# Sketched attention and a gated convolution on one core: loads in a set order, a new computing order, and no filler matmuls in TensorE's gaps

## The chip, the cores and the metric

The kernel runs on one core of one Trainium2 chip. The metric is the device time of one execution in microseconds. The kernel before takes 61.66 us in the median of three runs (61.4 to 61.86). The profile is one more execution of the same program; its span, from the first to the last instruction, is 60.0 us.

The core has five engines that run side by side, each in its own strict order: TensorE (PE, matmuls; PEld is its loading of weights), VectorE (DVE), ScalarE (ACT), GpSimd (POOL) and SyncE (SP, which here only issues transfers). ACT issues some transfers too.

## The reference

There are 4 batches, 4 heads, 1088 positions and 32 numbers a head. Keys and queries are taken to 64 features, the outer product of two projections to 8 numbers. Attention is linear: `kv` sums over all positions of a batch, so no query of a batch can be finished before all its keys and values are in. Batches don't depend on each other.

```python
def phi(x):                                     # (b, h, s, 32) -> (b, h, s, 64)
    a = einsum('rd,bhsd->bhsr', S1, x)
    b = einsum('rd,bhsd->bhsr', S2, x)
    return einsum('bhsi,bhsj->bhsij', a, b).reshape(*x.shape[:-1], 64)
q_p, k_p = phi(q), phi(k)
kv  = einsum('bhsf,bhsd->bhfd', k_p, v)         # sum over all positions
z   = sum(k_p, axis=2)
x   = einsum('bhsf,bhfd->bhsd', q_p, kv) / (einsum('bhsf,bhf->bhs', q_p, z) + 1e-6)
# x as (batch, 1088, 128): a causal convolution of 5 taps gives the gate
gate = sigmoid(sum(conv_w[t] * x[s - 4 + t] for t in range(5)))
out  = ((x @ w_val) * gate) @ w_out
```

## The kernel before

The program is a list of steps. Every step is a function of a kind, a batch and an index, and the list `ORDER` is the order in which they are emitted; each engine runs its own steps in that order. Digits after a colon choose among seven PSUM banks. The kinds are:

- `lk`, `lq`, `lv`, `lo`, `ls`, `lw`: loads of k, q, v, the last 64 positions of v of each batch (`v_lo`), S1 and S2, the weights. `cn`: constants.
- keys: `kt` (DVE transposes k), `kp` (PE projects it by S), `ke` (ACT copies the projection to SBUF), `kd` and `ko` (the outer product, on DVE and on POOL), `kv` (PE sums over the positions), `pz`, `pv`, `pm`, `pe` (kv and z made into weights for the queries).
- queries: `qt` (DVE transposes q), `qp` (PE projects), `qc` (ACT copies), `qm`, `qr`, `qi`, `qn` (the denominator and its division), `qo` (outer product, on DVE or POOL), `qx` (PE transposes phi), `qe` (copy to SBUF), `nm` (PE: times kv), `xe` (copy).
- gated part: `hl` (halo for the convolution), `gt` (PE: convolution by diagonal matrices), `sg` (ACT: sigmoid), `vl` (PE: times w_val), `gv` (DVE: gate times value), `om` (PE: times w_out), `oe` (copy), `so` (store).
- `cn06` and `zz`: matmuls of zeros by zeros, whose results nobody reads; `zz07:2` is seven of them.

```python
ORDER = """
cn08 lk01 cn00 ls00 cn06:01 lk00 lo00 ls01 lk10 cn05 cn07 lw00
cn09 lk20 kt01 lv12 lv01 zz07:2 lv02 cn01 lv00 cn02 lv03 kt00
cn013 cn011 cn010 kp00:2 kt10 lq01 lo01 kp01:3 ke00 cn03:4 zz05:0 ke01
ko00 cn04 lk30 kd01 kp10:5 lv13 kp11:6 lv10 ko01 ke10 kd00 kt20
... # cut
"""
...
elif i == 6:                                    # cn06
    for t in range(9):
        mm(bank("cn", b, i, t % 2), zero[:, 0:P], zero)

def s_zz(b, i):
    for t in range(i):
        mm(bank("zz", b, i), zero[:, 0:P], zero)

def queue(kind, b, i):                          # which engine issues a transfer
    return nc.scalar if (kind, b, i) in ON_ACT else nc.sync

def load(kind, b, i, x, y, t0, n):
    queue(kind, b, i).dma_start(
        out=y[b][:, t0 * D : (t0 + n) * D],
        in_=x[b].rearrange("h (m t) d -> (h m) (t d)", m=M)[:, t0 * D : (t0 + n) * D],
    )
# k and q of batch 0 come in two transfers (256 and 288 KB), of the others in one (544 KB);
# v in four of 128 KB a batch.

def s_kt(b, u):                                 # batch 0 in two halves, the others at once
    ...
    nc.vector.transpose(o, i_)

def s_kp(b, u):                                 # PE: wq[0] holds S1 and S2, spread over the heads
    ... mm(o[64 * z : 64 * z + 64, :, c, :], lt, wq[0][:, 0:64])

def s_kd(b, u):                                 # DVE does the first KD[b][u] of 4 + u chunks
    if KD[b][u]:
        outer(nc.vector, b, u, 0, KD[b][u], kab_view(b, u))

def s_ko(b, u):                                 # POOL does the others
    if KD[b][u] < 4 + u:
        outer(nc.gpsimd, b, u, KD[b][u], 4 + u, kab[(2 * b + u) % 4])

def copy(kind, b, i, out, in_):                 # qe, xe and oe
    if (kind, b, i) in ON_DVE:
        nc.vector.tensor_copy(out=out, in_=in_)
    else:
        nc.scalar.copy(out=out, in_=in_)
...                                             # cut: QM_POOL, QN_POOL, QO_POOL choose POOL or DVE likewise
for item in ORDER:
    what, _, banks = item.partition(":")
    kind, b, i = what[:2], int(what[2]), int(what[3:])
    slot[kind, b, i] = [int(x) for x in banks]
    steps["const" if kind == "cn" else kind](b, i)
```

Transfers share eight completion semaphores, dealt out in the order of the list. A transfer is issued only when the one eight places before it has landed, and while it waits, the issuing engine's later instructions wait with it.

Of the kernel before, what the change touches and what calls it, by code (L numbers as in the profile page):

```python
# [24 lines left out]


ORDER = """
cn08 lk01 cn00 ls00 cn06:01 lk00 lo00 ls01 lk10 cn05 cn07 lw00
cn09 lk20 kt01 lv12 lv01 zz07:2 lv02 cn01 lv00 cn02 lv03 kt00
cn013 cn011 cn010 kp00:2 kt10 lq01 lo01 kp01:3 ke00 cn03:4 zz05:0 ke01  # L30
ko00 cn04 lk30 kd01 kp10:5 lv13 kp11:6 lv10 ko01 ke10 kd00 kt20
lv11 lq00 kv00 ko10 ke11 lq10 zz01:0 lw02 kv01 lw01 kd10 kd11
kp20:0 ko11 pv00 kp21:1 pz00 kt30 lq20 ke20 zz02:2 ko20 lv20 kv10
lv22 ke21 lv21 kv11 qt00 lv23 ko21 pm00:2 kd20 kd21 qt01 pv10
kp30:4 pz10 pe00 qt10 lv33 pm10:3 ke30 qp01:5 lv31 pe10 lq30 kd30
cn012 kp31:6 qc01 qp11:0 lv32 qm01 ke31 qt20 ko30 lv30 qp00:1 qc11
ko31 qr01 kv20 qc00 kd31 kv21 qi01 qm00 qm11 qn01 qr00 qp10:2
qo03 pz20 pv20 qi00 qt30 pm20:3 qn00 qc10 qx03:4 kv30 qo01 pe20
qe03 qm10 kv31 qr10 qi10 qp20:6 qo02 pz30 pv30 qn11 qo00 qx01:5
qn10 qo13 qx02:3 qc20 pm30:2 qo11 qe01 qp21:4 qm20 qe02 pe30 qx00:1  # L40
qo12 nm03:6 qc21 qx13:5 qe00 nm02:3 qo10 qm21 qp30:2 xe02 qr20 qe13
nm00:0 qi20 qp31:1 qc30 xe00 qn20 xe03 qx10:3 qm30 nm01:5 qc31 qx12:0
qe10 qo20 nm13:6 xe01 qx11:2 qm31 xe13 nm10:3 gt00:51 qr30 qe12 hl00
qn21 xe10 qe11 qo21 gt01:60 sg00 qi30 sg01 vl02:3 qo23 vl00:2 sg03
nm12:5 qx20:1 sg02 gv00 nm11:0 qn31 xe12 qx23:4 gv02 qx21:6 xe11 qo22
qe23 vl03:2 vl01:5 qe21 gt10:30 gv01 hl10 gv03 nm23:4 qn30 sg11 om00:65
qe20 qx22:2 qo33 sg10 xe23 vl11:0 oe02 nm20:1 vl10:3 oe00 qe22 om01:5
so04 nm21:4 gv10 xe20 nm22:2 qo31 qx33:6 oe01 so00 xe21 gt11:31 so01
gv11 so02 gt20:45 sg12 xe22 qo30 sg13 so03 qe33 vl13:0 vl12:3 sg20
om10:21 gv13 sg21 qx31:6 gv12 qo32 oe12 qx30:4 oe10 qe31 nm33:0 so14  # L50
vl20:5 vl21:1 xe33 om11:3 gv20 nm31:2 so11 qe30 hl20 qx32:6 oe11 gt21:05
xe31 so10 qe32 gv21 hl30 nm30:4 so12 sg23 vl23:2 om20:36 xe30 sg22
nm32:1 so13 vl22:5 oe22 oe20 gt30:04 gv22 so24 gv23 so20 vl30:6 xe32
vl31:3 sg30 om21:5 so21 sg31 gt31:21 gv30 oe21 gv31 vl33:0 vl32:4 sg33
so22 om30:65 sg32 gv33 so23 oe30 gv32 oe32 om31:31 so30 so31 oe31
oe33 so34 so32 so33
""".split()


# [1 line left out]
def kernel(  # L61
# [25 lines left out]
    def st(name, shape, dt=F32):  # L87
        return sb.tile(shape, dt, tag=name, name=name)
# [23 lines left out]
    xe = [st(f"xe{i}", [P, 4 + NT, M], BF16) for i in range(3)]  # L112
# [163 lines left out]
    def kab_view(b, u):  # L276
        return bank("kp", b, u)[:, 0 : 2 * (4 + u) * 32].rearrange("p (k c x) -> p k c x", k=2, c=4 + u)
# [125 lines left out]
    def s_qn(b, U):  # L403
        pool = (b, U) in QN_POOL
        n = 4 * (5 - U)
        (nc.gpsimd if pool else nc.vector).tensor_mul(
            an[b % 2][:, rows(U), :], qa(b, U, 0, pool), bc(den[b % 2][:, rows(U)], 2, [P, n, 8])
        )

    def s_qo(b, g):  # L410
        U = g // 2
        lo = 8 * (g % 2)
        n = 12 if g == 1 else 8
        pool = (b, g) in QO_POOL
        a_ = an[b % 2][:, 20 * U + lo : 20 * U + lo + n, :]
# [95 lines left out]
    def s_so(b, g):  # L511
# [11 lines left out]

    KD = [[0, 4], [0, 3], [0, 0], [3, 2]]
    QM_POOL = {(0, 1), (1, 1)}
    QN_POOL = {(0, 0), (1, 0), (2, 0), (3, 0), (3, 1)}
    QO_POOL = {
        (0, 1), (0, 2), (0, 3), (1, 0), (1, 1), (2, 0), (2, 1), (2, 2), (3, 0), (3, 1), (3, 2), (3, 3),  # L530
    }
    ON_DVE = {
# [3 lines left out]
    }  # L536
    ON_ACT = {
        ('lk', 0, 0), ('lk', 0, 1), ('lk', 1, 0), ('lq', 0, 1), ('lv', 0, 2), ('lv', 0, 3),
        ('lv', 1, 1), ('lv', 1, 2), ('lw', 0, 2), ('so', 0, 1), ('so', 2, 4), ('so', 3, 0),
        ('so', 3, 2),  # L540
    }
    steps = {n[2:]: f for n, f in locals().items() if n.startswith("s_")}
# [35 lines left out]
```

## Time and profile before

| | before |
|---|---|
| time, median of 3 runs | 61.66 us |
| span of the profile | 60.0 us |
| PE busy | 47.5 us, 79% |
| weight loads (PEld) | 36.6 us, 61% |
| DVE busy | 39.5 us, 66% |
| ACT busy | 28.8 us, 48% |
| POOL busy | 35.4 us, 59% |
| read from HBM | 6.85 MB |
| written to HBM | 2.23 MB |
| zero matmuls on PE | 24, 8.3 us busy, 493 ns each |

The page gives busy time by engine, then cuts the span into 40 slices of 1.5 us and gives for each engine the share that it was busy, in tenths; PEclk is the clock granted to TensorE. The chain of waits follows the work that ended last back to what released it. The windows give busy time by engine for stretches that one chooses. Matmul records overlap one another, so their starts are a better measure than their lengths. A matmul of f32 leaves two records.

### The profile page before, as it was taken

The numbers are of one execution on the slowest core, as the hardware profiler recorded it, in microseconds if no ns is written. First come the engines' busy times: TensorE is split into PE (matmuls) and PEld (weight loads), VectorE is DVE, ScalarE is ACT, GpSimd is POOL, SyncE is SP. The second block draws the span as 40 slices with busy tenths as digits, with TensorE's granted clock in tenths as the row PEclk, the third lists the DMA queues.
The fourth block names the chain that finished last, engine by engine and source line by source line (L and its number), as shares of the span: only waits on it lengthen the run. The fifth ranks groups of instructions, "written<-read, shape, count | busy, mean of one in ns | idle before, by whom it ended". The sixth has DMA issues, their size and how long they took to land.

```text
span 60.0 us, 2668 instructions
## 1 busy us (share of the span) xinstructions
PE 47.5 (79%) x1129; PEld 36.6 (61%) x1129; DVE 39.5 (66%) x88; ACT 28.8 (48%) x83; POOL 35.4 (59%) x62
## 2 busy tenths in 40 slices
PE   1999709999704699999999999999999999962000
PEld 0333108587501687899888889988699797731000
DVE  1053089995399406696698796898799899964000
ACT  0540004940530005536356298999686999792000
POOL 4980052998399980008999988499999921000000
PEclk9999999999999555579999999999999999999955
DMA  0798999989999759300000000000000843897960
GB/s 0 195 285 277 352 340 262 256 282 358 404 378 340 225 146 376 126 0 0 11 0 0 11 0 5 11 5 0 16 0 22 262 116 82 193 238 164 242 186 3
DMA packets 6998, 9.25 MB, mean 154 GB/s; under 512 B 2117, under 2 KB 4682, under 8 KB 6986
## 3 DMA queue, kind: packets, MB, share of 16 engines
q1 hardware_dynamic: 5370, 6.69, 36.9%
q10 hardware_dynamic: 1616, 2.39, 13.0%
q8 instruction: 9, 0.15, 0.9%
q14 instruction: 3, 0.02, 0.1%
HBM read 6.85 MB, written 2.23 MB: 151 GB/s over the span
## 4 chain that ended last, share of the span: by engine, by line
PE 56%; DMA 29%; SPq 2%; ACTq 2%; ACT 2%; issue 1%
PE ring L140 36%; DMA q_in<-in_q_dram 11%; PE kv L140 9%; DMA s2raw<-in_S_dram 9%; DMA v_in<-in_v_dram 9%; PE ring L431 8%; PE ring L343 2%; ACT osb L231 2%; SPq L238 1%; ACTq L257 1%; SPq L263 1%; ACTq L519 1%
## 5 line engine op out<-in xcount | busy, mean ns | idle before, releaser
L417 POOL TENSOR_TENSOR phi<-an,abc 128x512 bf16<-128x512 f32 (+1 forms) x12 | 14.4, 1217 | 0.7 <-PE ring L140 0.3
L294 POOL TENSOR_TENSOR phik<-kab 128x1024 f32<-128x1024 f32 (+4 forms) x8 | 11.9, 1513 | 2.6 <-ACT kab L288 2.5
L140 PE MATMUL ring<-zero 128*128 128x512 bf16 x24 | 8.3, 493 | 3.6 <-issue 2.3
L272 DVE STREAM_TRANSPOSE kT<-k_in 128x1024 f32<-128x1024 f32 (+1 forms) x5 | 8.3, 1656 | 2.5 <-DMA k_in<-in_k_dram 2.5
L140 PE MATMUL ring<-wq,qT 128*64 128x96 f32 x144 | 7.9, 262 | 0.0
L288 ACT COPY kab<-ring 128x256 f32<-128x256 f32 (+1 forms) x8 | 3.1, 400 | 9.7 <-PE ring L140 9.7
L477 DVE TENSOR_TENSOR gv<-gate,ring 128x256 bf16<-128x256 bf16 x16 | 6.5, 441 | 1.5 <-PE ring L140 0.7
L140 PEld LDWEIGHTS <-zero 128*128 128x128 bf16 x24 | 2.7, 121 | 7.7 <-issue 5.6
L140 PE MATMUL kv<-phik,v_in 128*32 128x64 f32 x256 | 6.5, 244 | 0.9 <-DMA v_in<-in_v_dram 0.9
L140 PEld LDWEIGHTS ring<-wq,qT 128*64 128x64 f32 x144 | 6.8, 146 | 0.5 <-ACT kab L288 0.2
L140 PE MATMUL ring<-wq,kT 128*64 128x64 f32 x144 | 5.7, 235 | 1.8 <-POOL wq L201 1.8
L140 PEld LDWEIGHTS ring<-wq,kT 128*64 128x64 f32 x144 | 5.1, 148 | 3.0 <-POOL wq L201 2.3
L431 PE MATMUL ring<-ident,phi 128*64 128x128 bf16 (+1 forms) x144 | 6.7, 218 | 0.0
L140 PEld LDWEIGHTS kv<-phik,v_in 128*32 128x32 f32 x256 | 5.3, 124 | 1.8 <-DMA v_in<-in_v_dram 1.1
L466 ACT ACTIVATE gate<-ring 128x256 bf16<-128x256 f32 (+1 forms) x16 | 5.4, 400 | 1.8 <-PE ring L140 1.5
L140 PE MATMUL ring<-xe,diag 64*64 64x256 bf16 (+1 forms) x160 | 6.1, 279 | 0.0
L431 PEld LDWEIGHTS <-phi 128*64 128x64 bf16 (+1 forms) x144 | 5.5, 109 | 0.6
L380 ACT COPY abc<-ring 128x480 f32<-128x480 f32 (+2 forms) x8 | 4.2, 519 | 2.8 <-PE ring L140 2.8
L231 ACT COPY phiT<-ring 128x512 bf16<-128x512 bf16 (+1 forms) x8 | 5.1, 635 | 0.2 <-PE ring L431 0.2
L357 DVE STREAM_TRANSPOSE qT<-q_in 128x1088 f32<-128x1088 f32 (+2 forms) x5 | 5.2, 1050 | 0.0
L294 DVE TENSOR_TENSOR phik<-ring,kab 128x768 f32<-128x768 f32 (+2 forms) x4 | 3.8, 942 | 2.1 <-ACT kab L288 2.1
L338 ACT COPY kvf<-kv 128x128 f32<-128x128 f32 x4 | 1.1, 266 | 8.1 <-PE kv L140 5.8
(64 smaller groups left out, 80.3 us busy)
## 6 DMA issues: line engine op xcount, KB each, us to landing
out_dram<-osb SPq DMA_DIRECT2D x13, 128.0 KB, 2.4
q_in<-in_q_dram SPq DMA_DIRECT2D x3, 544.0 KB, 6.8
v_in<-in_v_dram SPq DMA_DIRECT2D x12, 128.0 KB, 3.7
k_in<-in_k_dram SPq DMA_DIRECT2D x2, 544.0 KB, 5.8
k_in<-in_k_dram ACTq DMA_DIRECT2D x1, 544.0 KB, 5.7
v_in<-in_v_dram ACTq DMA_DIRECT2D x4, 128.0 KB, 4.3
out_dram<-osb ACTq DMA_DIRECT2D x3, 128.0 KB, 2.4
k_in<-in_k_dram ACTq DMA_DIRECT2D x1, 288.0 KB, 2.9
```

Of the source, the lines that this page charges most:

```text
L140: nc.tensor.matmul(o, lhsT=lhsT, rhs=rhs, start=start, stop=stop, skip_group_check=True, **kw)
L231: nc.scalar.copy(out=out, in_=in_)
L272: nc.vector.transpose(o, i_)
L288: nc.scalar.copy(out=kab[(2 * b + u) % 4][:, :, 0 : 4 + u, :], in_=kab_view(b, u))
L294: eng.tensor_mul(phik[(2 * b + u) % 4][:, c0:c1].rearrange("p c h (i j) -> p (c h) i j", i=r), bc(a_, 3, [P, n, r, r]), bc(b_, 2, [P, n, r ...
L343: nc.tensor.transpose(o[:, 64:192], kvf[b].rearrange("p x f -> p (x f)"), ident32)
L357: nc.vector.transpose(flat(qT[b % 3][:, t0 : t0 + n, :]), q_in[b][:, t0 * D : (t0 + n) * D])
L380: nc.scalar.copy(out=abc[(2 * b + U) % 4][:, k0:3, 0 : 32 * ns], in_=bank("qp", b, U)[:, 32 * ns * k0 : 96 * ns].rearrange("p (k x) -> p k ...
L417: (nc.gpsimd if pool else nc.vector).tensor_mul(phi[g][:, 0:n, :].rearrange("p c (i j) -> p c i j", i=r), bc(a_, 3, [P, n, r, r]), bc(b_, ...
L431: nc.tensor.transpose(o[64 * (h % 2) : 64 * (h % 2) + 64, h // 2, c * P : c * P + n], phi[g][:n, 4 * c + h, :], ident[:n, :n],)
L466: nc.scalar.activation(out=gate[g][:, 0:n], in_=bank("gt", b, g // 2, g % 2)[:, 0:n], func=ACT.Sigmoid)
L477: nc.vector.tensor_mul(o[:, 0:512].rearrange("p (c w m j) -> p w j c m", c=4, w=2, m=M)[:, w], view(gate[g]), view(vl))
```

## The change

The list is replaced by another. What it does:

- Loads: k of batch 0 goes out first, one half on each issuing engine, and S1 and S2 directly behind it; then v, k, `v_lo` and q, batch by batch, in a fixed order, all but four of them on SP. Before, S1 is SP's first transfer, S2 its third behind `v_lo`, and k of batches 1 and 2 goes out ahead of v of batch 0.
- Computing: a batch's queries begin sooner after its keys; kv, qp and qx of the first batches stand earlier in the list. The shares of the engines (`KD`, the three POOL sets, `ON_DVE`) are set anew for it. The last unit to be computed is the first half of batch 3 and no longer the second.
- Zero matmuls: the nine of `cn06` at the start stay; the fifteen of the four `zz` steps go.

It is for starting TensorE's work on a batch as soon as that batch's data are in, instead of when most loads are through.

```diff
 ORDER = """
-cn08 lk01 cn00 ls00 cn06:01 lk00 lo00 ls01 lk10 cn05 cn07 lw00
-cn09 lk20 kt01 lv12 lv01 zz07:2 lv02 cn01 lv00 cn02 lv03 kt00
-cn013 cn011 cn010 kp00:2 kt10 lq01 lo01 kp01:3 ke00 cn03:4 zz05:0 ke01
-ko00 cn04 lk30 kd01 kp10:5 lv13 kp11:6 lv10 ko01 ke10 kd00 kt20
-lv11 lq00 kv00 ko10 ke11 lq10 zz01:0 lw02 kv01 lw01 kd10 kd11
-kp20:0 ko11 pv00 kp21:1 pz00 kt30 lq20 ke20 zz02:2 ko20 lv20 kv10
-lv22 ke21 lv21 kv11 qt00 lv23 ko21 pm00:2 kd20 kd21 qt01 pv10
-kp30:4 pz10 pe00 qt10 lv33 pm10:3 ke30 qp01:5 lv31 pe10 lq30 kd30
-cn012 kp31:6 qc01 qp11:0 lv32 qm01 ke31 qt20 ko30 lv30 qp00:1 qc11
+cn08 lk01 cn00 lk00 cn06:01 ls01 ls00 lv00 lv01 cn05 lv02 lv03
+cn09 cn07 kt01 lk10 lo00 cn01 cn02 lo01 kt00 cn013 lq01 cn011
+cn010 lq00 kp00:2 lk20 kp01:3 ke00 lv10 kd00 ko00 ke01 lv11 ko01
+kd01 kv00 lv12 kt10 lv13 lq10 kv01 lw00 qt01 lw01 kp10:4 pv00
+pz00 qt00 pm00:5 ke10 kp11:6 pe00 kd10 ko10 lw02 kt20 qp01:0 ke11
+lk30 qp00:1 lv20 qc01 ko11 lv21 kv10 qc00 kd11 lv22 qm01 kp20:2
+qm00 qr01 lv23 kv11 qr00 ke20 qi01 cn012 qi00 lq20 qn01 kp21:3
+qt10 lv30 pv10 ko20 lv31 pz10 lv32 kd20 qo02 pm10:4 lv33 kt30
+ke21 qo03 qx02:5 cn03:6 pe10 lq30 kv20 qe02 ko21 cn04 qx03:2 qp10:0
+kd21 qn00 kp30:4 qo01 kp31:5 qe03 qo00 qc10 qt20 kv21 ke31 qm10
 ... # cut: the rest of the list, with the same steps in another order
-so22 om30:65 sg32 gv33 so23 oe30 gv32 oe32 om31:31 so30 so31 oe31
-oe33 so34 so32 so33
+oe22 oe20 gv33 so24 gv32 vl31:2 sg30 vl30:5 om31:43 so21 sg31 gv30
+oe33 gv31 so20 oe31 so32 om30:06 so33 oe32 oe30 so34 so30 so31
 """.split()
-    KD = [[0, 4], [0, 3], [0, 0], [3, 2]]
-    QM_POOL = {(0, 1), (1, 1)}
-    QN_POOL = {(0, 0), (1, 0), (2, 0), (3, 0), (3, 1)}
-    QO_POOL = {
-        (0, 1), (0, 2), (0, 3), (1, 0), (1, 1), (2, 0), (2, 1), (2, 2), (3, 0), (3, 1), (3, 2), (3, 3),
-    }
+    KD = [[3, 1], [1, 3], [0, 1], [4, 0]]
+    QM_POOL = {(0, 0), (0, 1), (1, 0), (2, 0), (3, 0), (3, 1)}
+    QN_POOL = {(1, 0), (1, 1), (2, 0), (3, 0)}
+    QO_POOL = {(0, 0), (0, 3), (1, 0), (1, 3), (2, 1), (2, 2), (3, 0), (3, 1), (3, 2), (3, 3)}
     ON_DVE = {
-        ('oe', 0, 1), ('oe', 1, 1), ('oe', 2, 2), ('oe', 3, 1), ('oe', 3, 2), ('qe', 0, 2),
-        ('qe', 1, 0), ('qe', 1, 1), ('qe', 2, 0), ('qe', 2, 2), ('qe', 2, 3), ('qe', 3, 1),
-        ('qe', 3, 3), ('xe', 0, 0), ('xe', 2, 2), ('xe', 2, 3), ('xe', 3, 0), ('xe', 3, 2),
+        ('oe', 1, 0), ('oe', 1, 1), ('oe', 2, 2), ('oe', 3, 2), ('qe', 1, 3), ('qe', 2, 1),
+        ('qe', 2, 3), ('qe', 3, 1), ('qe', 3, 2), ('qe', 3, 3), ('xe', 1, 2), ('xe', 3, 2),
     }
     ON_ACT = {
-        ('lk', 0, 0), ('lk', 0, 1), ('lk', 1, 0), ('lq', 0, 1), ('lv', 0, 2), ('lv', 0, 3),
-        ('lv', 1, 1), ('lv', 1, 2), ('lw', 0, 2), ('so', 0, 1), ('so', 2, 4), ('so', 3, 0),
+        ('lk', 0, 1), ('ls', 0, 0), ('lv', 0, 1), ('lv', 0, 3), ('so', 1, 4), ('so', 3, 0),
         ('so', 3, 2),
     }
```

More of the change, by code (lines that the diff above doesn't have):

```diff
@@ L36 @@
-cn012 kp31:6 qc01 qp11:0 lv32 qm01 ke31 qt20 ko30 lv30 qp00:1 qc11
[L37 to L51, printed above, removed]
@@ L52 @@
-xe31 so10 qe32 gv21 hl30 nm30:4 so12 sg23 vl23:2 om20:36 xe30 sg22
-nm32:1 so13 vl22:5 oe22 oe20 gt30:04 gv22 so24 gv23 so20 vl30:6 xe32
-vl31:3 sg30 om21:5 so21 sg31 gt31:21 gv30 oe21 gv31 vl33:0 vl32:4 sg33
-so22 om30:65 sg32 gv33 so23 oe30 gv32 oe32 om31:31 so30 so31 oe31
-oe33 so34 so32 so33
+cn08 lk01 cn00 lk00 cn06:01 ls01 ls00 lv00 lv01 cn05 lv02 lv03
+cn09 cn07 kt01 lk10 lo00 cn01 cn02 lo01 kt00 cn013 lq01 cn011
+cn010 lq00 kp00:2 lk20 kp01:3 ke00 lv10 kd00 ko00 ke01 lv11 ko01
+kd01 kv00 lv12 kt10 lv13 lq10 kv01 lw00 qt01 lw01 kp10:4 pv00
@@ new lines @@
+pz00 qt00 pm00:5 ke10 kp11:6 pe00 kd10 ko10 lw02 kt20 qp01:0 ke11
[4 more added lines that the diff above has]
+kd21 qn00 kp30:4 qo01 kp31:5 qe03 qo00 qc10 qt20 kv21 ke31 qm10
+ke30 qp11:3 ko31 pv20 kd31 pz20 kd30 pm20:6 qc11 qx01:1 pe20 nm03:2
+qx00:5 qm11 nm02:4 xe03 qp20:6 qr10 xe02 qe00 qi10 ko30 kv30 qt30
@@ new lines @@
+qe01 qn10 qn11 kv31 qc20 qo13 qo12 nm01:2 pv30 qp21:4 pz30 xe01
+qo11 qm20 nm00:5 hl00 pm30:1 qc21 qo10 gt01:32 xe00 qm21 pe30 qr20
+gt00:05 sg03 qi20 sg02 vl03:1 qn21 qn20 qx11:2 sg01 gv03 qx13:3 sg00
+qx12:5 qo21 qe11 qx10:1 qo23 qp30:0 qe12 qe13 qo20 qe10 vl00:2 nm13:4
+qo22 vl02:3 qp31:5 qc30 gv00 xe13 gv02 vl01:1 nm10:6 qc31 qm30 nm12:2
+gv01 nm11:0 om01:4 xe10 qm31 qx21:3 xe12 xe11 om00:16 oe01 qr30 gt10:20
+hl10 oe02 qi30 so03 oe00 qe21 gt11:46 qn30 sg11 so04 qn31 sg10
+vl11:1 qo31 qx20:3 sg12 so01 qx23:0 gv11 sg13 qx22:5 qe20 vl12:2 qe23
@@ new lines @@
+so02 vl10:4 vl13:6 nm21:1 gv12 qe22 nm23:0 qo33 so00 nm20:3 gv10 qx31:2
+xe23 gv13 nm22:5 xe21 om10:40 qe31 xe22 om11:6 hl20 qx33:1 oe12 oe10
+qo32 xe20 gt21:52 so14 qe33 so10 gt20:03 oe11 sg22 qo30 sg23 so11
+qx32:4 sg21 nm31:1 so12 vl23:5 qe32 sg20 vl22:6 qx30:2 xe31 gv23 vl21:3
+so13 nm32:0 qe30 vl20:4 gv22 hl30 nm33:1 xe32 xe33 om21:5 nm30:6 gv21
+gt31:21 oe21 gv20 xe30 vl32:0 so23 om20:35 sg33 vl33:4 sg32 so22 gt30:61
+oe22 oe20 gv33 so24 gv32 vl31:2 sg30 vl30:5 om31:43 so21 sg31 gv30
+oe33 gv31 so20 oe31 so32 om30:06 so33 oe32 oe30 so34 so30 so31
```

## The prediction

> **What bounds the kernel now.** I read the page's slices first, then the chain of waits, then the windows of five microseconds, then TensorE's timeline from 15 us on and the end of the timeline. The slices of 1.5 us each:
>
> ```profile
> span 60.0 us, 2668 instructions
> PE   1999709999704699999999999999999999962000
> DVE  1053089995399406696698796898799899964000
> POOL 4980052998399980008999988499999921000000
> PEclk9999999999999555579999999999999999999955
> DMA  0798999989999759300000000000000843897960
> GB/s 0 195 285 277 352 340 262 256 282 358 404 378 340 225 146 376 126 0 0 11 0 0 11 0 5 11 5 0 16 0 22 262 116 82 193 238 164 242 186 3
> ```
>
> There are two halves. Until about 24 us the loads run (6.85 MB are read), TensorE has holes at slices 4, 10 and 11, and its clock drops to half in slices 13 to 17. From about 25 us no load is left and PE is at 9 in every slice until 52 us. The chain of waits says what set the start of the second half:
>
> ```profile
> 2.13 5.47 DMA s2raw<-in_S_dram
> 8.22 6.60 DMA q_in<-in_q_dram
> 14.85 5.15 DMA v_in<-in_v_dram
> 20.04 2.60 PE kv L140 x73
> ```
>
> (columns: start, length, what). Three transfers follow one another, each held by the one before, and only at 20.0 us does a chain of TensorE work begin that never stops again. The windows (PE, PEld, DVE, ACT, POOL busy, then clock and DMA share):
>
> ```profile
> 15.00:20.00 5.00, 1.79 (x34) 1.04 (x30) 4.10 (x6) 1.29 (x4) 4.06 (x3) 0.95 1.01 366
> 20.00:25.00 5.00, 4.96 (x116) 4.04 (x116) 1.59 (x4) 1.13 (x5) 2.33 (x5) 0.50 0.71 232
> 25.00:30.00 5.00, 5.00 (x165) 4.70 (x166) 3.97 (x8) 2.44 (x7) 2.86 (x4) 0.87 0.01 3
> 35.00:40.00 5.00, 5.00 (x125) 4.61 (x127) 4.22 (x13) 4.66 (x15) 4.06 (x6) 1.00 0.02 5
> ```
>
> From 15 to 20 us PE has next to nothing to do; from 20 to 25 us it is full but at half clock, and the three other engines wait for it (1.59, 1.13 and 2.33 of 5 us). After 25 us PE is full, with DVE and ACT close behind. So the time is: 20 us of loading with PE mostly idle, 6.3 us at half clock, 27.1 us of full PE (26.29 to 53.4), and an end of 5.4 us after PE's last matmul at 54.56. Halving shows in single rows of PE's timeline:
>
> ```profile
> 24.95 1.51 PE L140 MATMUL ring<-wq,qT 128*64 128x96 f32 x16
> 26.88 1.65 PE L140 MATMUL ring<-wq,qT 128*64 128x96 f32 x36
> ```
>
> 16 records take 1.34 us to the next start (84 ns each), later 36 take 1.58 us (44 ns each).
>
> **What the Trainium skill says.** "TensorE: Matmul & The Clock Gate", section "Part 1: The HAM clock gate": TensorE starts at half clock, is released after a busy window of about 3.4 us, and is throttled again after an idle one; the windows run freely. The trace agrees: the drop at 19.5 us and the return at 26.3 us are 6.8 us apart, two such windows, and PE's row for 15 to 20 us shows 1.79 us busy just before the drop. It also warns of judging PE by matmul busy time ("Perfetto Trace Analysis", section "Identifying the Most-Contended Engine": take the weight loads' share). Here PEld is 4.4 to 4.7 of 5 us from 25 to 40 us, so PE is nearly full by that measure as well. "DMA: Bandwidth & Descriptors", section "Issuing engines are not separate DMA queues": transfers of several issuing engines share the same 16 DMA engines and interleave. The trace agrees: s2raw, 16 KB, took 5.5 us, issued behind 1.09 MB of k on another engine's queue. So what counts is the order of the bytes, not who issues them.
>
> **The change, part by part.**
>
> *S and k first.* Before, kp of batch 0 starts at 8.94 us: S2 lands at 7.6, then its transpose (0.21), then the transpose of the second half of k that stands behind it in DVE's order (1.04, 7.76 to 8.80). After, k's halves go out first on two queues and S1, S2 straight behind: 0.59 MB, which the GB/s row has delivered at about 4.1 us. Then DVE has 1.04 + 0.20 + 0.16 + 0.21 + 1.04 = 2.65 us of transposes, so kp starts at about 7.0: 1.9 us earlier.
>
> *The chain of loads.* There are eight completion semaphores, so each load waits for the load eight places before it. With nearly all on one queue they land in order. By the same GB/s row, 0.52 MB of v and 0.56 of k or q each: v0 5.9, k1 7.5, v rest 7.9, q0 9.7, k2 11.9, v1 13.7, q1 15.2, weights 15.6, k3 17, v2 18.4, q2 20.3, v3 22, q3 23.5 us. I looked for bubbles: wherever a load waits, two or three more (0.8 to 1 MB, some 3 us) are still in flight, so none. The end of loading stays at 23 to 24 us; only the order gains. q0 comes at 9.7 instead of 16.4, k3 at 17 instead of 15.
>
> *The zero matmuls.* 15 of 24 go, the first 9 stay. They fill holes and are on no path, so their 15 x 0.43 us at half clock are not the gain. What they give up is the clock: with 9 of them PE is busy from 1.26 to about 5.1 us, less likely a whole window than the former 16 (to 7.1). I take the first 16 us or so as half clock.
>
> *The new order, by hand (estimates from the rows' lengths; PE at half clock at first).* kp0 7.0 to 9.2. ACT copy 0.4, then outer products: DVE 0.95, POOL 0.63 and 1.96. POOL ends at 12.0, kv of batch 0 at 13.2. k1's transpose on DVE ends at 12.7. From 13.2 PE has kp10, pm00, kp11, qp01, qp00: (36 x 60) + 0.9 + (36 x 84) ns = about 6.1 us, to 19.2. Then kv10, kp20, kv11, kp21 to about 22. That is 8.6 us without a hole, so a whole 3.4 us window lies in it and the full clock returns at about 17 to 20 instead of 26.3 us. From 22 to 26 PE waits for DVE, which is full in this stretch: q1's transpose (1.28), then zm and pm10 at about 23, phi (0.66), k3's transpose (2.25). With kv20, qp10, qx02, qx03 and kp30, PE stands at 26 us ahead of the kernel before by: 40 more records of qp x 44 ns = 1.8, 16 transposes x 28 ns = 0.45, half a kv = 0.75, together 3.0 us.
>
> *Split of the copies.* DVE has fewer evacuations (12 instead of 18, about -2.5 us) but more phi (4.56 instead of 2.6 us) and fewer pden: 38.6 instead of 39.5 us. POOL: phi 12 to 10 (-3.0), pden 2 to 6 (+1.95), 33.5 instead of 35.4. ACT takes over what DVE drops: 28.8 to about 31.7. All remain below PE.
>
> *The end.* The last unit is now U=0 of batch 3, copied by ACT in one piece (0.6 us). Before, the last store was ready at 55.03 but SP issued it only at 56.66, as SP's stores queue at about 0.6 us each:
>
> ```profile
> 54.66 0.37 ACT L231 COPY osb<-ring 128x256 f32<-128x256 f32 x1 [0.61 <-PE ring L140]
> 55.82 0.74 SPq L515 DMA_DIRECT2D out_dram<-osb_lo  x1
> 56.66 0.54 SPq L519 DMA_DIRECT2D out_dram<-osb  x1
> ```
>
> Stores start earlier after, and the last two go out on two engines: 0.1 + 0.6 + 0.05 + 0.55 issue + 1.8 landing + 1.0 closing = about 4.2 us instead of 5.4.
>
> *Sum.* 26.0 + (27.1 - 3.0) = 50.1 if PE stays full; I add 1.3 for waits, since an order with more dependent batches in flight will not be without holes: 51.4. Plus 4.2: a span of 55.6. Times stand 1.66 above the span (61.66 to 60.0): 57.3 us.
>
> **Rivals.** (1) The clock. If PE's work before 20 us is too broken for a whole busy window, half clock lasts to about 26 us as before, and the work from 17 to 26 us, some 6 us busy, moves back by about 3 us: 60 us, no gain to speak of. For it: the zeros are gone and the former kernel fell to half clock even with them. Against it: the stretch from 13.2 to 22 us. (2) DVE becomes the bound. It is busy almost without a break from 4.1 us, in strict order, with the long transposes (2.05 and 1.28 us) ahead of short ones that PE waits for. If every step of it slips, its 38.6 us and 5 us of holes end at about 48, gv last, and PE at 52: 58 to 59 us. (3) Loading is the bound anyway: q3 lands at 23.5 as before, and 544 KB of q for batch 3 must still pass transpose, qp, phi, qx, nm, gate and output. But that last batch's own PE work is a quarter of some 37 us, so 23.5 + 10 is far from the end; I give this little. (4) More is gained: holes in the second half do not come and the clock is released at about 6 us by the 9 zeros; then 55 us.
>
> **Range and chances.** Main line 57.3; rival 2 lifts it by 1 to 2, rival 1 by 3, rival 4 lowers it by 2. Range 54.7 to 60.6. Faster by 2% means under 60.4: 0.78. Same: 0.14. Slower than 62.9 needs the clock and the order to fail together: 0.08.
>
> **What would show it.** kp's first matmul near 7.0 instead of 8.94. The chain without s2raw at its head. q_in of batch 0 landing near 10. PEclk at full from slice 11 to 13 on, and no drop at 20 us. PE's slices filled from 9 on. The last matmul near 51, SP's last store issued within a microsecond after ACT's last copy. Wrong would be: PEclk at 5 to slice 17, holes in PE after 28 us with DVE or POOL full, or gaps in the DMA row before 22 us.

## The result and the profile after

| | before | after |
|---|---|---|
| time, median of 3 runs | 61.66 us (61.4 to 61.86) | 57.28 us (57.18 to 57.39) |
| ratio, with 95% interval | 1 | 0.929 (0.923 to 0.936) |
| span of the profile | 60.0 us | 55.4 us |
| PE's last matmul ends | 54.56 us | 50.28 us |
| busy: PE / DVE / ACT / POOL | 47.5 / 39.5 / 28.8 / 35.4 us | 44.3 / 38.6 / 31.4 / 33.7 us |
| zero matmuls | 24 | 9 |

The time falls by 4.4 us. The page's slices of after, 1.385 us each and counted from 0 in the text (before's were 1.5):

```profile
span 55.4 us, 2635 instructions
PE   0998093879999969898999999999999999962000
DVE  1006938499897699998699798889599969572000
POOL 4881609700876999999966994996699930000000
PEclk9999998555569999999999999999999999999985
DMA  0587899999999989964000000000225872877960
GB/s 0 146 288 253 225 293 173 293 413 368 335 292 332 286 259 331 288 244 163 15 0 12 6 0 12 0 6 6 53 54 133 196 182 67 188 170 169 233 190 0
```

PE is at 8 or 9 in nearly every slice from slice 9 on, that is from 12.5 us; before it was so from slice 14 on, 21 us, and there at half clock up to 26.3. The half clock now comes early, in slices 7 to 11, and is over at 16.1 us. The row PEclk shows full clock also where the trace has no record of the clock yet. After's records begin at 5.85 us, and the nine zeros ahead of that took 0.61 to 0.63 us each; before's shortest, at full clock, took 0.38. So PE was at half clock up to 5.85 us too. The loads have not become shorter: DMA is at 8 or 9 until 23.5 us and the last load lands near 26. PE simply no longer waits for the end of them.

The chain of waits (start, length, what) says what set the start of the uninterrupted work:

```profile
0.81 3.77 DMA k_in<-in_k_dram
4.60 5.81 DMA k_in<-in_k_dram
10.44 2.02 DVE kT L271
12.45 0.06 DVE kT L273
12.52 1.27 PE ring L139 x20
```

Two transfers of k, one transpose, and from 12.52 us PE's work; before there were three transfers one behind the other and the work began at 20.0. After that the chain goes through PE, except for one stretch in which ACT and POOL hold it up:

```profile
14.19 3.15 PE ring L139 x56
17.36 0.57 ACT abc L379
...
18.00 0.53 POOL pden L392
18.52 0.23 POOL wv L210
18.76 0.25 POOL wo L211
...
19.76 1.96 POOL phik L293
21.71 1.04 POOL phi L416
...
22.80 0.41 PE ring L430 x8
```

The windows (PE, PEld, DVE, ACT, POOL busy with counts, clock, DMA share, GB/s) show the same by engine:

```profile
15.00:20.00 5.00, 5.00 (x170) 4.54 (x168) 4.09 (x9) 2.10 (x5) 3.98 (x9) 0.89 0.95 298
20.00:25.00 5.00, 4.22 (x128) 3.53 (x122) 4.97 (x9) 3.95 (x13) 5.00 (x4) 1.00 0.89 288
25.00:30.00 5.00, 4.85 (x158) 4.06 (x157) 4.13 (x7) 3.49 (x12) 4.07 (x5) 1.00 0.12 45
35.00:40.00 5.00, 5.00 (x131) 4.51 (x129) 4.38 (x12) 4.77 (x14) 4.08 (x7) 1.00 0.04 10
```

Compare the first row with that of before: from 15 to 20 us PE starts 170 matmuls where it started 34, and 168 weight loads where it made 30. From 20 to 25 us PE is the one that waits (4.22 of 5), with DVE (4.97) and POOL (5.00) full. From 25 us on, all four engines are busy, and PE is full.

The end of the timeline (start, length, engine, line, what, idle before and who ended it):

```profile
49.53 0.75 PE L139 MATMUL ring<-wo,gv 128*64 128x128 bf16 x9 [0.39 <-DVE gv L476]
...
50.55 0.59 ACT L230 COPY osb<-ring 128x512 f32<-128x512 f32 x1 [0.71 <-PE ring L139]
50.84 0.60 SPq L514 DMA_DIRECT2D out_dram<-osb_lo  x1
51.16 0.54 ACTq L518 DMA_DIRECT2D out_dram<-osb  x1
51.53 0.56 SPq L518 DMA_DIRECT2D out_dram<-osb  x1
```

ACT's last copy ends at 51.14 us, SP issues the last store at 51.53, since it was still issuing the small one; the span ends at 55.4. PE's last matmul ends at 50.28 us, some 4.3 us earlier than before's:

```profile
54.15 0.41 PE L140 MATMUL ring<-wo,gv 128*64 128x128 bf16 x8 [0.73 <-DVE gv L477]
```

### The profile page after: what moved, and what is told of

It reads as the page before. It is cut to its first block, busy times and chain, and to the rows that moved or that the text cites. A ratio compares the mean times of both kernels' runs of the same rounds, so it can differ in the third digit from the quotient of the medians.

```text
span 55.4 us, 2635 instructions
## 1 busy us (share of the span) xinstructions
PE 44.3 (80%) x1114; PEld 35.1 (63%) x1114; DVE 38.6 (70%) x83; ACT 31.4 (57%) x89; POOL 33.7 (61%) x62
## 4 chain that ended last, share of the span: by engine, by line
PE 53%; DMA 17%; POOL 8%; DVE 5%; ACT 4%; issue 2%; ACTq 1%
PE ring L139 38%; DMA k_in<-in_k_dram 17%; PE ring L430 8%; PE kv L139 5%; DVE kT L271 4%; POOL phik L293 4%; POOL phi L416 2%; ACT osb L230 2%; PE ring L342 2%; DVE gv L476 1%; ACT gate L465 1%; ACTq L518 1%; ACT abc L379 1%; POOL pden L392 1%; POOL wo L213 1%
## 5 line engine op out<-in xcount | busy, mean ns | idle before, releaser
L416 POOL TENSOR_TENSOR phi<-an,abc 128x512 bf16<-128x512 f32 (+1 forms) x10 | 11.5, 1158 | 0.5 <-DVE gv L476 0.3
L139 PE MATMUL ring<-wq,kT 128*64 128x64 f32 x144 | 6.4, 248 | 2.1 <-POOL wq L200 1.8
L139 PEld LDWEIGHTS ring<-wq,kT 128*64 128x64 f32 x144 | 5.6, 159 | 3.6 <-POOL wq L200 2.6
L430 PEld LDWEIGHTS <-phi 128*64 128x64 bf16 (+1 forms) x144 | 5.0, 109 | 1.5 <-POOL phi L416 0.3
L230 ACT COPY phiT<-ring 128x512 bf16<-128x512 bf16 (+1 forms) x10 | 5.7, 620 | 0.0
L230 ACT CAST xe<-ring 128x256 bf16<-128x256 f32 (+1 forms) x14 | 5.3, 399 | 0.4 <-PE ring L139 0.3
L293 DVE TENSOR_TENSOR phik<-ring,kab 128x256 f32<-128x256 f32 (+2 forms) x6 | 4.2, 718 | 1.2 <-ACT kab L287 1.2
L139 PE MATMUL ring<-zero 128*128 128x512 bf16 x9 | 4.0, 631 | 1.3 <-DVE zero L220 1.3
L416 DVE TENSOR_TENSOR phi<-an,ring 128x512 bf16<-128x512 f32 (+1 forms) x6 | 4.6, 763 | 0.3 <-PE ring L430 0.2
```

The costliest lines, as they stand in the source:

```text
L139: nc.tensor.matmul(o, lhsT=lhsT, rhs=rhs, start=start, stop=stop, skip_group_check=True, **kw)
L293: eng.tensor_mul(phik[(2 * b + u) % 4][:, c0:c1].rearrange("p c h (i j) -> p (c h) i j", i=r), bc(a_, 3, [P, n, r, r]), bc(b_, 2, [P, n, r ...
L416: (nc.gpsimd if pool else nc.vector).tensor_mul(phi[g][:, 0:n, :].rearrange("p c (i j) -> p c i j", i=r), bc(a_, 3, [P, n, r, r]), bc(b_, ...
L430: nc.tensor.transpose(o[64 * (h % 2) : 64 * (h % 2) + 64, h // 2, c * P : c * P + n], phi[g][:n, 4 * c + h, :], ident[:n, :n],)
```

## The experiments

My theory was that the gain is one of order: PE gets at the early batches' work while the loads run, which needs the new loads, the new order of computing and the shares of the engines together. Its rivals: the loads alone do it; the clock does it (half clock early, where it costs less); the zero matmuls had cost time. Each run is beside runs of the kernel before on its own chip. A ratio is that of undisturbed executions alone, so it can differ from the quotient of the two medians; where none is given there were too few of them.

| run | what it is | median, us (range, runs) | before there, us | ratio (95%) |
|---|---|---|---|---|
| b_nozz | before, without its 15 zeros in gaps | 61.66 (59.43–62.47, 4) | 61.38 | none |
| b_loads_a | before, with after's loads | 62.08 (61.37–62.45, 4) | 61.38 | 1.023 (1.007–1.039) |
| a_loads_b | after, with before's loads | 60.46 (59.14–61.94, 20) | 61.38 | 0.999 (0.988–1.010) |
| a_zz | after, with 16 zeros more | 57.53 (56.86–58.16, 4) | 61.38 | 0.941 (0.927–0.956) |
| a_again | after, once more | 57.26 (56.13–59.17, 6) | 62.10 | 0.919 (0.902–0.937) |
| b_warm | before, with 9 zeros more | 61.12 (60.22–63.49, 6) | 62.10 | 0.988 (0.974–1.002) |
| a_slate | after, S behind v of batch 0 | 58.20 (57.05–60.82, 6) | 62.10 | 0.947 (0.934–0.960) |
| a_casts | after, weight casts later | 57.89 (56.74–58.19, 6) | 62.10 | 0.931 (0.911–0.951) |
| a_shares_b | after, with before's shares | 61.13 (60.27–62.45, 22) | 61.51 | none |
| a_no9 | after, without any zeros | 57.47 (55.95–58.37, 6) | 61.51 | none |
| a_k1 | after, k of batch 1 ahead of v | 58.80 (56.26–60.98, 6) | 61.51 | none |
| a_k1_act | a_k1, weight casts on ACT | 57.66 (56.16–60.31, 6) | 61.51 | none |

Runs scatter by 2 to 4 us here, more than the three of the first comparison. Differences under about 1 us are not read as such. Line numbers of the experiments differ by a few from those of after, because their lists are broken into fewer lines.

### The loads alone, in both directions

b_loads_a: before's computing, with the transfers in after's sequence (the small load of the convolution's weights moved up behind v of batch 0, and ON_ACT's loads those of after).

```diff
-cn08 lk01 cn00 ls00 cn06:01 lk00 lo00 ls01 lk10 cn05 cn07 lw00
-cn09 lk20 kt01 lv12 lv01 zz07:2 lv02 cn01 lv00 cn02 lv03 kt00
+cn08 lk01 cn00 lk00 cn06:01 ls01 ls00 lv00 lv01 cn05 cn07 lv02 cn09 lv03 kt01 lw00 lk10
+zz07:2 lo00 cn01 lo01 cn02 lq01 kt00 ...      # cut: computing as before, loads as after
```

> The kernel before (its computing order, shares and zeros) with the loads in the sequence and on the engines of the kernel after (the small gate-tap load moved up, since the order needs it early). My theory: the old order asks for k of batches 1 and 2 first, and these now land 3 to 5 us later, so the gain at the head is lost: 60.5 to 63 us. Rival 'the chain of loads alone makes the gain': 58.5 or less.

a_loads_b: after's computing, with the transfers in before's sequence (on ACT the halves of k of batch 0 and k of batch 1).

```diff
-cn08 lk01 cn00 lk00 cn06:01 ls01 ls00 lv00 lv01 cn05 lv02 lv03
+cn08 lk01 cn00 ls00 cn06:01 lk00 lo00 ls01 lk10 cn05 lw00 lk20 cn09 cn07 kt01 lv12 lv01 ...
-        ('lk', 0, 1), ('ls', 0, 0), ('lv', 0, 1), ('lv', 0, 3), ('so', 1, 4), ('so', 3, 0),
-        ('so', 3, 2),
+        ('lk', 0, 0), ('lk', 0, 1), ('lk', 1, 0), ('so', 1, 4), ('so', 3, 0), ('so', 3, 2),
```

> The kernel after with the loads in the sequence of the kernel before (S third, k of batches 1 and 2 ahead of v of batch 0, q of batch 0 late; all on SP but the first three k), its computing order and shares unchanged. My theory: order of loads and order of computing work together; kv and the queries of batch 0 come 2 to 4 us later, and since PE is full afterwards most of it stays: 59 to 61.5 us. Rival 'the new computing order and shares alone make the gain': 57.0 to 58.3.

Measured: 62.08 us, no better than before, and 60.46 us, some 3 us above after. In DVE's timeline of b_loads_a the old order meets the new loads: it asks for k of batch 3 ahead of q of batch 0.

```profile
19.81 1.99 DVE L265 STREAM_TRANSPOSE kT<-k_in 128x1024 f32<-128x1024 f32 x1 [3.60 <-DMA k_in<-in_k_dram]
...
21.77 1.31 DVE L350 STREAM_TRANSPOSE qT<-q_in 128x576 f32<-128x576 f32 x2
```

DVE stands for 3.60 us for that k, while q, which lies behind it in the list, is not touched until 21.8 us; in after q's transpose came at 12.4. In DVE's timeline of a_loads_b the new order meets the old loads, and the strict order of DVE makes two waits of it:

```profile
8.00 0.21 DVE L176 STREAM_TRANSPOSE sT<-s2raw 128x32 f32<-128x32 f32 x1 [3.10 <-DMA s2raw<-in_S_dram]
...
17.80 0.78 DVE L350 STREAM_TRANSPOSE qT<-q_in 128x576 f32<-128x576 f32 x1 [1.83 <-DMA q_in<-in_q_dram]
```

DVE stands for 3.10 us for S2, and for 1.83 us from 16 us on for q of batch 0, with k's outer product behind it. So neither the new loads without the new order, nor the new order with the old loads, brings the gain. That the loads alone do it, as a rival, is out. b_loads_a has the old shares too; the old order with the new shares was not run.

### The shares of the engines

a_shares_b: after's list and loads, with the four sets that say who does what as they were before.

```diff
-    KD = [[3, 1], [1, 3], [0, 1], [4, 0]]
-    QM_POOL = {(0, 0), (0, 1), (1, 0), (2, 0), (3, 0), (3, 1)}
-    QN_POOL = {(1, 0), (1, 1), (2, 0), (3, 0)}
+    KD = [[0, 4], [0, 3], [0, 0], [3, 2]]
+    QM_POOL = {(0, 1), (1, 1)}
+    QN_POOL = {(0, 0), (1, 0), (2, 0), (3, 0), (3, 1)}
...                                             # cut: QO_POOL and ON_DVE likewise
```

> The kernel after with the shares of DVE, POOL and ACT (KD, the POOL sets, the copies on DVE) as in the kernel before, its order and loads unchanged. My theory: the order was made for its shares; with the others DVE has 18 instead of 12 evacuations, in strict order at places that were not meant for them: 58 to 60 us. Rival 'the shares are of no account': within 0.4 us of the kernel after.

Measured 61.13 us in 22 runs: nearly the whole gain goes, more than I expected. DVE's timeline shows one long wait, PE's shows two:

```profile
25.96 0.69 DVE L416 TENSOR_TENSOR phi<-an,ring 128x512 bf16<-128x512 f32 x1 [2.90 <-POOL an L405]
```

```profile
22.18 0.41 PE L430 MATMUL ring<-ident,phi 128*64 128x128 bf16 x8 [1.32 <-POOL phi L416]
...
28.83 0.31 PE L139 MATMUL ring<-zm,s2rep 128*64 128x32 f32 x4 [1.45 <-DVE zm L330]
```

```profile
20.00:25.00 5.00, 3.39 (x104) 2.96 (x106) 2.62 (x5) 2.86 (x12) 5.00 (x4) 1.00 0.89 297
25.00:30.00 5.00, 3.55 (x109) 2.79 (x107) 4.04 (x7) 2.41 (x9) 4.90 (x6) 1.00 0.08 31
```

With before's shares one more outer product of the queries of batch 0 is POOL's (the `phi` that PE waits for at 22.18 us; in after DVE does it at 20.68), and so is the normalization `an` of a unit of them. In POOL's list both stand behind long outer products. DVE waits 2.90 us for `an`, then its other work is late and PE waits for zm. In the two windows PE is busy 3.39 and 3.55 of 5 us; with after's shares it was 4.22 and 4.85. The difference, 2.1 us, is more than half of the 3.8 us lost; where the rest went was not followed. From 20 to 25 us POOL is full in both kernels: the total of its work says nothing of this, what stands ahead of what does.

### The zeros and the clock

b_nozz: before, with its list stripped of the four `zz` steps.

```diff
-cn09 lk20 kt01 lv12 lv01 zz07:2 lv02 cn01 lv00 cn02 lv03 kt00
+cn09 lk20 kt01 lv12 lv01 lv02 cn01 lv00 cn02 lv03 kt00
...                                             # cut: zz05:0, zz01:0 and zz02:2 likewise
```

> The kernel before with its 15 gap-filling zero matmuls left out and nothing else changed. My theory: they lie in holes, so their own time is on no path, and the half clock that follows without them falls in a stretch that the loads set anyway: 61.2 to 62.4 us, ratio 0.99 to 1.01. Rival 'the zeros were a cost': 60.5 us or less. Rival 'the zeros held the clock up': half clock begins at about 9 us, and the time rises by over 1 us, to 62.7 or more.

a_zz: after, with zeros put ahead of four groups that come after waits.

```diff
-cn010 lq00 kp00:2 lk20 kp01:3 ke00 lv10 kd00 ko00 ke01 lv11 ko01
-kd01 kv00 lv12 kt10 lv13 lq10 kv01 lw00 qt01 lw01 kp10:4 pv00
+cn010 lq00 zz07:0 kp00:2 lk20 kp01:3 ke00 lv10 kd00 ko00 ke01 lv11 ko01
+kd01 zz04:0 kv00 lv12 kt10 lv13 lq10 zz03:0 kv01 lw00 qt01 lw01 zz02:0 kp10:4 pv00
```

> The kernel after with 16 zero matmuls put back into its early holes (7 after the first 9, 4 between the key projections and kv of batch 0, 3 within that kv, 2 before the next key projection). The clock should then stay full from 5.8 us on instead of falling to half from 9.3 to 16.1 us. My theory: kv of batch 0 and the stretch from 12.5 to 16.1 us go at double speed, but DVE's transposes and POOL's outer products set most of that stretch, so the gain is 0.3 to 1.5 us (55.8 to 57.0). Rival 'PE's early clock doesn't matter': within 0.3 us of 57.3. Rival 'zeros in gaps block real work in PE's strict order': 57.6 or more.

a_no9: after, without the nine zeros at the start, so without any.

```diff
-cn08 lk01 cn00 lk00 cn06:01 ls01 ls00 lv00 lv01 cn05 lv02 lv03
+cn08 lk01 cn00 lk00 ls01 ls00 lv00 lv01 cn05 lv02 lv03
```

> The kernel after without its first nine zero matmuls, so with none at all. Theory 'TensorE's clock before 16 us is of no account to the new order': within 0.4 us of the kernel after, with half clock from the start to some 17 us. Rival 'the nine matter, they give a full clock for the first key projections': 0.8 us or more above it.

b_warm: before, with more zeros in the gaps in which its clock had dropped.

```diff
-lv11 lq00 kv00 ko10 ke11 lq10 zz01:0 lw02 kv01 lw01 kd10 kd11
-kp20:0 ko11 pv00 kp21:1 pz00 kt30 lq20 ke20 zz02:2 ko20 lv20 kv10
+lv11 lq00 kv00 ko10 ke11 lq10 zz05:0 lw02 kv01 lw01 kd10 kd11
+kp20:0 ko11 pv00 kp21:1 pz00 kt30 lq20 ke20 zz07:2 ko20 lv20 kv10
```

> The kernel before with its third and fourth zero steps made larger (5 and 7 matmuls instead of 1 and 2), so that TensorE's clock is not halved at 19.5 us. My theory: half clock from 20 to 26 us costs the kernel before 2 to 3 us, as everything waits for PE there: 58.5 to 59.8 us, which leaves 1.5 to 2.5 us of the change's gain to order alone. Rival 'the half clock costs nothing, as in the kernel after': 61 us or more.

Measured: 61.66, 57.53, 57.47 and 61.12 us. The first three differ from the kernel that they come from by 0.3 us or less. The clock rows of a_zz and of a_no9:

```profile
PEclk9999999999999999999999999999999999999955
```

```profile
PEclk9999999999656999999999999999999999999996
```

The rows can't be read alone, as was said above. PE's first projection of k tells what the clock was: in after, in a_again (after once more, see below) and in a_no9 it is

```profile
7.03 1.27 PE L139 MATMUL ring<-wq,kT 128*64 128x64 f32 x36 [1.75 <-POOL wq L200]
...
7.03 2.19 PE L139 MATMUL ring<-wq,kT 128*64 128x64 f32 x36 [1.76 <-POOL wq L200]
...
7.20 2.19 PE L132 MATMUL ring<-wq,kT 128*64 128x64 f32 x36 [7.20 <-POOL wq L193]
```

After had full clock there, the two others half. Their records of the clock begin later: at 16.67 us in a_again, and at 11.15 in a_no9, which had full clock from there to 14.56 and half again to 17.97. So a high mean clock can also mean that the half clock went unrecorded (a_again's is 0.988), and the three executions of after, with mean clocks of 0.922, 0.989 and 0.987 and spans of 55.4 us each, don't say what the clock is worth. The two traces say more: a_again, at half clock up to 16.67 us, has a span of 55.5 us; after, with full clock from 5.85 to 9.26 us, has 55.4.

In a_zz the clock is full from 4.87 us on, and the time is that of after (57.28, and 57.26 again). I had expected a gain of 0.3 to 1.5 us, and the medians show none. But the half clock is not free on the way. POOL begins the second outer product of the keys of batch 2 at 21.85 us in a_zz and at 22.70 in after, and PE begins the kv that needs it, in a_zz and then in after, at

```profile
24.25 0.30 PE L133 MATMUL kv<-phik,v_in 128*32 128x64 f32 x4
...
25.02 0.32 PE L139 MATMUL kv<-phik,v_in 128*32 128x64 f32 x8
```

So a_zz is 0.77 us ahead at this point. Inside this kv PE then pauses, 0.64 us in a_zz and 0.15 in after (last section), and a_zz's lead is 0.29 us from there to the start of the last matmuls (49.24 against 49.53). DVE and POOL do wait for PE in the first 16 us; at the end this is worth about 0.3 us in these two traces, less than the scatter.

In b_warm the profiled execution ran at full clock from 7.15 us on and had a span of 58.5 us, 1.5 less than before's; the median was 1 us below before's, with 1 inside the interval. I had expected a gain of 2 to 3 us. In its profile PE begins the second part of the projection of k of batch 3 at 23.16 us, in before's at 26.29; of these 3.1 us, 1.8 are left at the start of the last matmuls (52.38 against 54.15), and two pauses of 0.55 and 0.45 us, of the kind of the last section, lie on the way. So the half clock at 20 to 26 us cost before about 1 us by the medians and 1.5 by the two spans. The first may be too low: the other five executions of b_warm had mean clocks of 0.919 to 0.955, below this one's 0.970, so more half clock was left in them. That the clock makes the whole gain is out all the same: b_warm, before's order with full clock from 7.15 us on, has a span of 58.5 us, and a_again, after's order at half clock up to 16.67 us, has 55.5. These 3 us are left to loads, order and shares; a finer split was not measured. Nor did the zeros cost before anything that can be seen: without them b_nozz takes 61.66 us, and before beside it 61.38.

### What stands first in the chain

a_slate: S1 and S2 behind v of batch 0, both on SP.

```diff
-cn08 lk01 cn00 lk00 cn06:01 ls01 ls00 lv00 lv01 cn05 lv02 lv03
+cn08 lk01 cn00 lk00 cn06:01 lv00 lv01 cn05 lv02 lv03 ls01 ls00
-        ('lk', 0, 1), ('ls', 0, 0), ('lv', 0, 1), ('lv', 0, 3), ('so', 1, 4), ('so', 3, 0),
+        ('lk', 0, 1), ('lv', 0, 1), ('lv', 0, 3), ('so', 1, 4), ('so', 3, 0),
```

> The kernel after with S1 and S2 issued behind v of batch 0 instead of ahead of it. They should land at 7 to 7.5 us as in the kernel before, and the first key projection start 2 us later, at about 9. My theory: DVE has some 1 us of slack before k of batch 1 lands at 10.4, the rest goes through: 57.8 to 58.8 us. Rival 'all of the head start counts': 59.0 or more. Rival 'the head is hidden behind the loads': within 0.3 us of the kernel after.

a_k1: k of batch 1 directly behind S, ahead of v of batch 0, because the chain of after goes through that k. a_k1_act: the same, with the casts of the weights on ACT and not on POOL.

```diff
-cn08 lk01 cn00 lk00 cn06:01 ls01 ls00 lv00 lv01 cn05 lv02 lv03
-cn09 cn07 kt01 lk10 lo00 cn01 cn02 lo01 kt00 cn013 lq01 cn011
+cn08 lk01 cn00 lk00 cn06:01 ls01 ls00 lk10 lv00 lv01 cn05 lv02 lv03
+cn09 cn07 kt01 lo00 cn01 cn02 lo01 kt00 cn013 lq01 cn011
```

```diff
-            nc.gpsimd.tensor_copy(out=wv, in_=wv_f)
+            nc.scalar.copy(out=wv, in_=wv_f)       # in a_k1_act alone; wo likewise
```

> The kernel after with k of batch 1 issued directly behind S, ahead of v of batch 0. In the kernel after DVE stands idle from 9.45 to 10.44 us until k of batch 1 has landed, and is then busy without a break to 26 us. If DVE's chain from that landing sets the end, it starts about 1 us earlier and the time falls by 0.5 to 1 us, to 56.3 to 56.8. Rival 'v of batch 0 is as urgent': kv of batch 0 moves back and nothing is gained. Rival 'POOL and PE's own fetching of instructions bound that stretch': within 0.3 us.

> As the run with k of batch 1 ahead of v of batch 0, and the four casts of the weights done by ACT, which has holes at 18 to 21 us, instead of POOL. If POOL's 1.2 us there bound as soon as DVE comes earlier: another 0.3 to 0.8 us less than that run, 55.6 to 56.4. Rival: no difference to that run.

a_casts: the casts of the weights on POOL (0.23 + 0.25 + 0.30 us in after's chain, from 18.52 us) later in the list, behind the outer product of batch 3.

```diff
-qm00 qr01 lv23 kv11 qr00 ke20 qi01 cn012 qi00 lq20 qn01 kp21:3
+qm00 qr01 lv23 kv11 qr00 ke20 qi01 qi00 lq20 qn01 kp21:3
-ke30 qp11:3 ko31 pv20 kd31 pz20 kd30 pm20:6 qc11 qx01:1 pe20 nm03:2
+ke30 qp11:3 ko31 cn012 pv20 kd31 pz20 kd30 pm20:6 qc11 qx01:1 pe20 nm03:2
```

> The kernel after with POOL's four casts of the weights (1.2 us) moved from the chain that its profile shows (18.47 to 19.69 us, ahead of the outer product that kv of batch 2 waits for) to a later hole of POOL. If that chain sets when PE becomes full, 56.1 to 56.8 us. Rival: DVE and PE's own work stand just as late there, and the time stays within 0.3 us of the kernel after.

a_again was after once more, beside a_slate, a_casts and b_warm.

> The kernel after, unchanged, as the measure for the others on this chip. Its three first executions had spans of 55.4 us each at mean clocks of 0.922, 0.987 and 0.989. If its time does not hang on TensorE's early clock, as these say, it stays at 57.0 to 57.6 us whatever clock is shown. If that was chance, it spreads by 2 us with the clock, as the kernel before does.

Measured: a_again 57.26; a_slate 58.20, a_k1 58.80, a_k1_act 57.66, a_casts 57.89. None beats after; a_k1, a_k1_act and a_casts were expected to. a_again's median is where I expected it, but its six executions run from 56.13 to 59.17 us, not from 57.0 to 57.6, and not in the order of their mean clocks (56.13 at 0.944, 57.33 at 0.988, 59.17 at 0.879). The three equal spans of the first comparison were in part chance; what makes the executions differ stays open. PE's timelines of a_slate and a_k1 show when the first projection starts, which was 7.03 us in after:

```profile
8.23 1.82 PE L133 MATMUL ring<-wq,kT 128*64 128x64 f32 x36 [2.95 <-POOL wq L194]
...
8.38 2.19 PE L133 MATMUL ring<-wq,kT 128*64 128x64 f32 x36 [3.11 <-POOL wq L194]
```

a_slate's loses 1.2 us at the start. Its median is 0.9 above a_again's, but the profiled execution had a span of 54.6 us, less than after's, with full clock from 12.1 us on (after's: from 16.1): between nothing and 1 us of it reaches the end, and the scatter doesn't let me say which. a_k1 was meant to bring k of batch 1 earlier. It does: k lands near 8.8 us, not at 10.4. But S1, though issued ahead of it, comes later here; the head of the chain of waits:

```profile
1.25 5.70 DMA s1raw<-in_S_dram
```

In this execution the 16 KB of S1 took 5.70 us, and what is won on k of batch 1 is lost on batch 0. It was the slowest of the six (60.98 us), and PE has a pause of 1.16 us in it besides. a_k1_act has the same list of loads; there S1 was used at 5.5 us, S2 took 4.83 us, and the first projection started at 7.43. S2 took 4.4 us in after and 3.5 in a_again, the same kernel. So the landing of S varies from one execution to the next, and that the 544 KB behind it hold it up is not shown.

In a_casts the 0.8 us of casts leave POOL's critical stretch, but POOL begins the outer product behind them no earlier: at 19.90 us, where after had 19.76. It now waits 0.59 us for ACT's copy of the projection. And the halo copy that stands behind the casts in their new place comes late: the first convolution starts at 32.85 us instead of 32.33, after a wait of 0.29 us for it. Taking work from one engine of the chain brought nothing, because the next one stood just as late.

## Why the prediction was right

57.3 us was predicted and 57.28 measured. The mechanism held in the main. Several sizes were off and cancelled, so that the sum hits within 0.1 us is luck.

- *S and k first: right.* The first projection of k starts at 7.03 us (7.0 predicted, 8.94 before), and the former head of the chain, s2raw, is gone from it. a_loads_b and a_slate show that it hangs on this order: 9.33 and 8.23 us. The parts were a little off: the first half of k landed at 4.58 us, not 4.1, and DVE's transposes took 2.27 us, not 2.65.
- *The chain of loads: the landing times were mis-sized.* k1 landed at 10.41 us, not 7.5; q0 near 12.2, not 9.7; k3 at 19.5, not 17; the end was near 26, not 23.5. I took the bytes over time from the GB/s row of before, but the new sequence moved only 225, 293 and 173 GB/s in slices 4 to 6, with the DMA engines at 8 or 9 all the while. There were no bubbles, as I had said; the bytes themselves went more slowly. Why is open: v, in pieces of 128 KB, now takes the place of k at 544 KB there, but no run separated piece size from the rest. DVE waited 0.99 us for k1; in its timeline from there to 26 us no other wait on a load stands, so that is all that can be seen of what the lateness cost.
- *The zeros: right that they are off the path, the price over-rated.* I counted the loss of the clock as a price. The medians of b_nozz, a_zz and a_no9 show none; a_zz's trace shows 0.77 us of it at 25 us and about 0.3 at the end. Two readings were wrong and change nothing: not all 15 ran at half clock (the five at 10.29 us took 1.25 us together), and PE's holes before are in slices 5, 11 and 12, not 4, 10 and 11.
- *The clock: right in time, mis-sized in worth.* Full from 16.1 us (17 to 20 predicted, 26.3 before). The Trainium skill, "TensorE: Matmul & The Clock Gate", section "Part 1: The HAM clock gate", gives free-running windows of about 3.4 us; after's record agrees: full clock from 5.85 to 9.26 us (3.41), half until 16.09 (6.83, two windows), the last of them filled by the work that begins at 12.5. What rival 1 put at 3 us is indeed 3.1 us in b_warm's trace at 23 to 26 us, but only 1 to 1.5 us of it reach the end.
- *The order by hand: right in shape, the lead was under-sized.* kv of batch 0 ended at 12.1 us (13.2 predicted), the first queries' projection at about 17.3 (19.2). DVE full from 20 to 25 us was predicted for 22 to 26. At 26.0 us PE had 24.3 us left to its last matmul's end; before, 28.3 from 26.29. So the lead, with all waits in it, was 4.0 us; the prediction had 3.0 less 1.3 for waits, 1.7. An early sign is pm10, which came at 20.8 us and not at 23. Of these 2.3 us a slip of my sum hid 1.2: it took before's full stretch to 53.4 us, but the last matmul ended at 54.56. So PE ended at 50.28 us instead of 51.4.
- *The split of the copies: right in the sums, under-rated as a cause.* DVE 38.6, ACT 31.4, POOL 33.7 us, against 38.6, 31.7, 33.5. I took the new shares for bookkeeping, worth something only through these sums. a_shares_b shows that without them the order is worth 0.4 us (61.13 against 61.51), which is within the scatter.
- *The end: mis-sized.* 5.1 us, not 4.2, after PE's last matmul. SP's last store is issued 0.4 us after ACT's copy, well within the microsecond that was named as a sign, but lands 2.8 us after its issue began, not 0.55 + 1.8.
- *Sum:* 1.1 us less for PE, 0.9 more for the end, and 0.2 more between span and time (1.88 against 1.66).
- *Rivals:* half clock to 26 us did not happen. DVE as the bound did, but only from 20 to 25 us. Loading as the bound did not: the last load came 2.5 us later than thought and nothing waited for it in the chain. Rival 4 came half true: PE was busy 4.85 to 5.00 of 5 us from 25 to 45 us, so hardly a hole came in the second half, but the clock, released at 5.85 us, stayed so for one window only.

## What to carry to other kernels

Loads, order and shares are one choice here: with engines in strict order, the new loads with the old order and shares, the new order and shares with the old loads, and the new loads and order with the old shares gave between +0.7 and -0.9 us, all three together -4.4. When TensorE's clock drops, ask who waits for PE at that moment and how much of the delay reaches the end: in before 3.1 us of it shrank to 1 to 1.5, in after 0.8 to 0.3. And check a clock row against the lengths of matmuls before it is believed. A small transfer that is issued first need not land early: the 16 KB of S1 took 5.70 us in one execution, and the same list had it there by 5.5 us of the span in another.

## What the runs showed of the hardware

In some traces PE stops at fixed places of its program. In PE's timeline of a_zz there are three pauses in which it waited for nothing that the profile shows:

```profile
15.62 0.54 PE L133 MATMUL ring<-wq,qT 128*64 128x96 f32 x6 [0.39 <-issue]
...
20.27 0.34 PE L133 MATMUL ring<-wq,kT 128*64 128x64 f32 x5 [1.30 <-issue]
...
25.19 0.25 PE L133 MATMUL kv<-phik,v_in 128*32 128x64 f32 x2 [0.64 <-issue]
```

They cut groups of equal matmuls in two, and fall at matmul records 222, 349 and 476 of PE, 127 apart. Before has one at 222 too, of 2.33 us, in the middle of its zeros:

```profile
18.50 0.39 PE L140 MATMUL ring<-zero 128*128 128x512 bf16 x1 [2.33 <-issue]
```

a_no9, with nine records fewer ahead of it, has a pause of 0.52 us at 476, and a_k1 and a_k1_act have pauses of 1.16 and 0.63 us at 476. Those of b_loads_a (0.47 us), b_nozz (0.66 and 0.91) and b_warm (1.31, 0.55 and 0.45) lie at such places too, or within three records of one. a_again, a_casts, a_slate, a_loads_b and a_shares_b have none. The page's list of DMA queues has a kind of its own for such traffic:

```profile
q8 instruction: 8, 0.13, 1.0%
```

Eight packets of 16 KB in after. In a_zz they start at 13.21, 17.39 and 22.58 us, and PE goes on 2.4 to 2.9 us later each time. I read it as PE's program being fetched in blocks, which come late when the loads fill the DMA engines. It was inferred from positions; no run was made to test it. What the traces do show is that a_zz lost most of its lead at such a place: 2.3 us of pauses stand in its loading phase, against 0.15 us at record 476 in after, and its lead of 0.77 us ahead of the one at 476 is 0.29 behind it. Without these pauses a_zz might have gained what I expected; no run shows it.
